# Alpha of the first four chunks loaded as two pairs, five staging tiles and fewer dummy matmuls in a fused linear attention and MLP kernel

## The chip, the core and the metric

The kernel runs on one core of one Trainium2 chip. The metric is the device time of one execution in microseconds (us); less is better. Several executions are timed and one more is profiled.

Engines are called as the profile calls them: PE (TensorE, matmuls; PEld is its weight loads), DVE (VectorE), ACT (ScalarE), POOL (GpSimd), SP (SyncE, which here issues every DMA from one queue, in program order). The on-chip memory has 128 partitions; matmul results go to PSUM banks.

## What is computed

A gated linear attention over 4 x 8 heads, 768 tokens and head width 48 feeds an MLP with a squared ReLU:

```python
B, H, S, D = q.shape            # 4, 8, 768, 48
state = np.zeros((B, H, D, D)); y = np.zeros_like(q)
for t in range(S):
    state = alpha[:, :, t, :, None] * state + np.einsum('bhd,bhe->bhde', k[:, :, t], v[:, :, t])
    y[:, :, t] = np.einsum('bhd,bhde->bhe', q[:, :, t], state)
x = y.transpose(0, 2, 1, 3).reshape(B * S, H * D)     # 3072 x 384
h = np.maximum(x @ w_in, 0.0)                         # w_in 384 x 2048
out = (h * h) @ w_out                                 # w_out 2048 x 384
```

All inputs and the output are float32.

## The kernel before

**Tiling.** The 3072 tokens are 24 chunks of 128, six per batch entry. Each chunk goes through the attention and becomes a block of 128 columns of `xT_big`; the MLP then works on groups of chunks (`GN`: the first group is chunks 0 to 3, then one, one, and pairs). Matmuls are bf16.

**A chunk of the attention** (`add_chunk`). The running product of alpha is a prefix sum of logarithms. ACT takes the logarithm; PE multiplies it with a triangular matrix (op `p0`, the prefix sums); ACT makes `A` = exp and `Ainv` = exp of the negative (L408, L412); DVE multiplies `qA` = q A (L431) and `kI` = k Ainv (L434); PE transposes both (`p1q`, `p1k`, L241); DVE or ACT copies them to `qkT`; PE forms the scores (`p2`, tile `sc`); DVE masks them (`sm`, L472, two halves); POOL has cast v to bf16 (`vb`, L388); PE multiplies scores with v and adds the state's part (`p3a`, `p3b`); ACT evacuates (`xn`), PE transposes (`p4`), and a copy writes `xT_big`. Beside that PE updates the state (`ps`), DVE scales it with `ae` (the exponential of the chunk's total logarithm, L492), ACT casts it (`sb`, L497). `p0`, the transposes, `p3` and `p4` share two PSUM banks (`GLA_BANKS`); the scores have one more tile.

**Alpha of the first four chunks** (`add_joint_alpha`, L312). The 512 tokens of chunks 0 to 3 are laid four to a partition: partition p holds tokens 4p to 4p+3, in pieces of 768 bytes per head. Two DMAs of four heads (L319) fill a tile taken from the staging pool; two logarithms (L324) write `L4`, a view of a tile that the MLP uses later. Chunk s then lies on partitions 32s to 32s+31, so its prefix sum is four matmuls on 32 rows with shifted windows of `tri4` (L397), and 16 small matmuls with `sel4` give the totals of all four chunks at once (`add_totals`, L334), from which two exponentials make `ae` (L342). All four prefix sums wait for both logarithms. From chunk 4 on, alpha is loaded, like q, k and v, as 128 tokens on 128 partitions in pieces of 192 bytes, 192 KB a load (L354).

**Weights** (`load_w`). w_in comes in six loads (cut at f-tiles 0, 2, 4, 6, 8, 12, 16 of 128 columns; 384 KB or 768 KB each), w_out in four of 768 KB. Each lands in a float32 staging tile (pool `stage`, four tiles, of which the joint alpha has one) and is cast to bf16 by POOL, DVE or ACT (L290 to L294). A load waits until the cast four places earlier in `w_cast` has freed its tile.

**MLP.** `add_moe1` makes blocks of 12 matmuls (in the first group: four f-tiles of one chunk, three contraction steps each), a ReLU on ACT (L577) and a square on DVE (L585); `add_moe2` makes four quarters of four f-tiles per chunk, each quarter of the first group needing one w_out load, then an evacuation (L617) and an output DMA.

**Order.** A planner (`Plan.run`) lists the operations with a duration, dependencies, a priority and the PSUM banks they take; it simulates the engines and sorts by planned start, and each engine's instructions are issued in that order. DMAs are one first-in first-out list, `DMA_ORDER`, with planned costs `LD` 0.98 us (chunk load), `JLD` 1.18 us (half of joint alpha), `WLD` 2.1 us (768 KB of weights) and a latency of 2.0 us; the first may start at 0.6 us. Other planned values: a logarithm of joint alpha 0.7 us, ACT's latency 0.14, slack ahead of PE 0.05. A chunk's `p0` may not run more than about three and a half chunks ahead of the MLP (`gate`).

**Dummies.** Until the second MLP layer starts, planned gaps on PE are filled with matmuls on a zero tile `warm`: seven 512 wide at the very start, planned to end at 4.2 us, and then, ahead of each PE operation, a number of 256-wide ones computed from the planned gap (L699), in 0.11 us each.

Of the kernel before, what the change touches and what calls it, by code (L numbers as in the profile page):

```python
# [11 lines left out]
ALU = mybir.AluOpType  # L12
# [127 lines left out]
def kernel(  # L140
# [36 lines left out]
    stage = ctx.enter_context(tc.tile_pool(name="stage", bufs=4))  # L177
# [19 lines left out]
    JN, JP = 4, 32  # L197
    JW = P + JN - 1
    tri4 = consts.tile([P, 192], BF16)
    sel4 = consts.tile([P, 64], BF16)  # L200
    nc.gpsimd.memset(tri4, 1.0)
    nc.vector.memset(sel4, 1.0)
    for c in range(JN):
        blk = slice(JP * c, JP * c + JP)
        nc.gpsimd.affine_select(
            out=tri4[blk, 0:JW], in_=tri4[blk, 0:JW], compare_op=ALU.is_ge, fill=0.0,
            base=-(JN - 1), pattern=[[1, JW]], channel_multiplier=-JN,
        )
    for c in range(JN):
        blk = slice(JP * c, JP * c + JP)  # L210
        nc.vector.memset(sel4[blk, 0:JN], 0.0)
        nc.vector.memset(sel4[blk, c:c + 1], 1.0)
# [18 lines left out]
    L4 = gT_s[:, 0:8, :].rearrange("p (r h) (a d) -> p r (h a) d", r=JN, a=4)  # L231
    nc.gpsimd.memset(L4[:, :, :, D:], 0.0)

# [32 lines left out]
    W_CUT = {"i": [0, 2, 4, 6, 8, 12, 16], "o": [0, 4, 8, 12, 16]}  # L266
    SB = 4
# [39 lines left out]
    EARLY = 4  # L307

    JLD = 1.18
    J = {}  # L310

    def add_joint_alpha():  # L312
        src = alpha[0, :, 0:JN * P, :].rearrange("h (p r) d -> p h (r d)", r=JN)
        hs = [slice(0, H // 2), slice(H // 2, H)]

        def ld(hf):
            if hf == 0:
                J["at"] = stage.tile([P, H, JN * D], FP32, name="at4", tag="stage")
            pin(nc.sync.dma_start(out=J["at"][:, hs[hf], :], in_=src[:, hs[hf], :]))  # L319
        lds = [add("DMA", JLD, lambda hf=hf: ld(hf), lat=2.0, at=0.6) for hf in range(2)]  # L320

        def e_ln(hf):
            t = J["at"][:, hs[hf], :].rearrange("p h (r d) -> p h r d", r=JN)
            pin(nc.scalar.activation(L4[:, :, hs[hf], 0:D].rearrange("p r h d -> p h r d"), t, AF.Ln))  # L324
        J["ln"] = [add("ACT", 0.7, lambda hf=hf: e_ln(hf), lds[hf], prio=-15.0) for hf in range(2)]
        w_cast.append(J["ln"][-1])
        add_totals()

    def add_totals():
        def e_tot():  # L330
            J["tot"] = psum(tot, [P, 512], FP32)
            for p in range(NP):
                for r in range(JN):
                    mm(J["tot"][:, JN * p:JN * (p + 1)], lhsT=L4[:, r, 2 * p:2 * p + 2, :], rhs=sel4[:, 0:JN],  # L334
                       start=(r == 0), stop=(r == JN - 1), skip_group_check=True)
        tot = Op("PE", 0.42, e_tot, J["ln"], prio=-9.9, takes=GLA_BANKS, lat=0.05)
        plan.add(tot)

        def e_ae(j):
            rows = slice(64 * j, 64 * j + 64)  # L340
            t = J["tot"][rows, 0:NP * JN].rearrange("p (n c) -> p c n", c=JN)
            pin(nc.scalar.activation(ae_s[rows, 0:JN, :, j], t, AF.Exp))  # L342
        x0 = add("ACT", 0.19, lambda: e_ae(0), tot, prio=-9.9)
        J["ae"] = add("ACT", 0.19, lambda: e_ae(1), tot, after(x0), prio=-9.9)
        tot.gives = J["ae"]
# [12 lines left out]
    def add_chunk(s):  # L358
# [16 lines left out]
        joint = s < JN  # L375
        jb = slice(JP * s, JP * s + JP)
# [3 lines left out]
        if joint:  # L380
            ln = J["ln"]
        else:
            ln = [add("ACT", 0.41, e_ln, d["ld_at"], old, prio=-15.0 if s < EARLY else -5.0)]
            d["use_at"] = ln[0]
# [7 lines left out]
        def e_p0():  # L392
            pm = d["pm"] = psum(p0, [P, 512], FP32)
            if joint:
                for r in range(JN):
                    mm(pm[:, 0:HD], lhsT=tri4[jb, JN - 1 - r:JN - 1 - r + P], rhs=L4[jb, r, :, 0:D],
                       start=(r == 0), stop=(r == JN - 1))  # L397
                return
# [4 lines left out]
        p0 = Op("PE", 0.66 if joint else 0.27, e_p0, ln, takes=GLA_BANKS, lat=0.05, **g)  # L403
# [18 lines left out]
        if joint:  # L422
            ae1 = J["ae"]
# [6 lines left out]
        def e_qA():  # L430
            pin(nc.vector.tensor_mul(qA[:, :, 0:D], d["qt"], d["A"]))  # L431

        def e_kI():
            pin(nc.vector.tensor_mul(kI[:, :, 0:D], d["kt"], d["Ai"]))  # L434
        mq = d["use_qt"] = add("DVE", 0.47, e_qA, a_, d["ld_qt"], old, **g)
        mk = d["use_kt"] = add("DVE", 0.47, e_kI, ai, d["ld_kt"], old, **g)
# [32 lines left out]
        def e_sm(hh):  # L469
            if hh == 0:  # L470
                d["sm"] = work.tile([P, 2, NP, P], BF16, name="sm")
            pin(nc.vector.tensor_mul(d["sm"][:, hh], d["sc"][:, hh], utri_b.to_broadcast([P, NP, P])))  # L472
        sm0 = add("DVE", 0.6, lambda: e_sm(0), p2, **g)
        sm1 = add("DVE", 0.6, lambda: e_sm(1), p2, after(sm0), **g)
        p2.gives = sm1
# [150 lines left out]
    DMA_ORDER = ["at", (0, "qt"), (0, "kt"), (1, "qt"), (1, "kt"), (0, "vt"), (2, "qt"),  # L626
# [108 lines left out]
```

## Time and profile before

| | us |
|---|---|
| median of 3 timed runs | 191.19 (190.68 to 192.44) |
| profiled execution | 192.79 |
| its span on the core | 191.1 |
| PE busy in the span | 183.5 |
| of it, dummies (57 matmuls, bank<-warm) | 11.5 |
| DVE busy / ACT busy | 128.0 / 123.8 |
| DMA queue, mean share of 16 engines | 66.6% |

The costliest groups on PE are the two MLP layers: 720 matmuls into the first layer (76.8 us busy) and 384 of the second (71.6 us). Busy time of matmuls counts each from issue to its modelled end, and they overlap, so the start-to-start distance is what one costs in a dense run.

"Idle before" and "releaser" name how long an engine sat idle before a group and what ended the wait. Numbers after "x" are counts. A DMA's line on SP is the time its issue took; the transfer lands some microseconds later. The granted clock (PEclk) is in shares of full speed.

Durations used later: a chunk's qA or kI 0.55 us on DVE; one half of the masked scores 0.68; a joint logarithm 0.84 us on ACT; A or Ainv 0.50; a weight cast of 768 KB 0.95 us on DVE, 1.47 on ACT; of 384 KB 0.55 and 0.83.

### The profile page before, as it was taken

What the parts mean: (1) busy time and instruction counts of PE and PEld (TensorE: products, weight loads), DVE (VectorE), ACT (ScalarE), POOL (GpSimd) and SP (SyncE); (2) the same over time, 40 slices, a digit from 0 to 9 for tenths busy, and PEclk for the clock granted to TensorE, in tenths of its full rate; (3) what the DMA queues carried; (4) which work ended last, traced back from release to release, by engine and by line L of the source; (5) the groups of instructions that cost most, each with busy time, mean ns of one, the idle gap of its engine ahead of it and who ended that gap; (6) DMA issues with size and microseconds to landing.
All of it is one profiled execution on the core that took longest, in us unless ns stands there. A gap on an engine that the chain in (4) does not pass through costs nothing.

```text
span 191.1 us, 5257 instructions
## 1 busy us (share of the span) xinstructions
PE 183.5 (96%) x2101; PEld 138.8 (73%) x2101; DVE 128.0 (67%) x277; ACT 123.8 (65%) x285; POOL 18.9 (10%) x43
## 2 busy tenths in 40 slices
PE   7898999889999999999999999999999999999992
PEld 2577899557886788857868868868868768768651
DVE  1178899654898999858758768767857858735100
ACT  4475799346896778946955955946946746728221
POOL 8121100101111111112110110010010000000000
PEclk9999999999999999999999999999999999999999
DMA  6999898999989999999999999650110110111112
GB/s 182 212 232 274 282 282 191 284 310 186 229 183 224 217 198 199 224 180 223 191 231 238 177 232 196 129 151 0 46 41 0 46 41 5 41 41 45 38 51 78
DMA packets 104730, 30.23 MB, mean 158 GB/s; under 512 B 96257, under 2 KB 103937, under 8 KB 104705
## 3 DMA queue, kind: packets, MB, share of 16 engines
q1 hardware_dynamic: 104704, 29.89, 66.6%
q8 instruction: 16, 0.26, 0.6%
q14 instruction: 10, 0.07, 0.1%
HBM read 25.17 MB, written 4.72 MB: 156 GB/s over the span
## 4 chain that ended last, share of the span: by engine, by line
PE 82%; DMA 8%; ACT 3%; DVE 2%; SPq 2%; issue 1%; POOL 0%; POOLq 0%
PE bank L238 69%; PE bank L241 7%; PE sc L238 4%; DMA wo<-in_moe_w_out_dram 3%; DMA at<-in_alpha_dram 2%; DMA vt<-in_v_dram 2%; SPq L354 2%; PE st L238 2%; DVE gT L585 1%; DVE w_out_b L292 1%; ACT r L577 1%; DVE w_in_b L292 0%; ACT ob L617 0%; ACT qkT L369 0%; ACT L_s L379 0%
## 5 line engine op out<-in xcount | busy, mean ns | idle before, releaser
L238 PE MATMUL bank<-xT_big,w_in_b 128*128 128x256 bf16 (+1 forms) x720 | 76.8, 251 | 0.0
L238 PE MATMUL bank<-w_out_b,gT 128*128 128x384 bf16 x384 | 71.6, 326 | 1.2 <-DVE w_out_b L292 1.2
L577 ACT ACTIVATE r<-bank 128x512 bf16<-128x512 f32 x96 | 56.4, 603 | 16.5 <-PE bank L238 14.2
L238 PEld LDWEIGHTS <-w_in_b 128*128 128x128 bf16 x720 | 55.5, 98 | 5.0
L238 PEld LDWEIGHTS <-gT 128*128 128x128 bf16 x400 | 35.6, 97 | 20.2 <-issue 1.2
L585 DVE TENSOR_TENSOR gT<-r 128x512 bf16<-128x512 bf16 x96 | 38.8, 429 | 14.6 <-ACT r L577 14.4
L472 DVE TENSOR_TENSOR sm<-sc,utri_b 128x512 bf16<-128x512 f32 x48 | 30.8, 683 | 3.3 <-PE sc L238 3.3
L388 POOL CAST vb<-vt 128x384 bf16<-128x384 f32 x24 | 14.2, 592 | 121.6 <-DMA vt<-in_v_dram 71.7
L431 DVE TENSOR_TENSOR qA_s<-qt,A 128x384 bf16<-128x384 f32 x24 | 13.3, 552 | 19.1 <-ACT A L408 19.1
L617 ACT COPY ob<-bank 128x384 f32<-128x384 f32 x23 | 11.0, 478 | 22.3 <-PE bank L238 22.2
L371 DVE COPY qkT<-bank 128x1024 bf16<-128x1024 bf16 (+1 forms) x23 | 15.0, 655 | 6.5 <-PE bank L241 6.5
L238 PEld LDWEIGHTS <-qkT 64*128 64x128 bf16 (+1 forms) x272 | 10.9, 95 | 6.8 <-issue 2.0
L408 ACT ACTIVATE A<-bank 128x384 bf16<-128x384 f32 x24 | 11.9, 497 | 4.9 <-PE bank L238 4.7
L434 DVE TENSOR_TENSOR kI_s<-kt,Ainv 128x384 bf16<-128x384 f32 x24 | 14.8, 615 | 0.2 <-DMA kt<-in_k_dram 0.2
L497 ACT CAST sb<-st 128x384 bf16<-128x384 f32 x20 | 9.6, 479 | 7.4 <-DVE st L492 7.3
L379 ACT ACTIVATE L_s<-at 128x384 bf16<-128x384 f32 x20 | 10.4, 522 | 5.8 <-DMA at<-in_alpha_dram 5.7
L238 PE MATMUL bank<-warm 128*128 128x256 bf16 (+1 forms) x57 | 11.5, 346 | 1.3 <-DVE warm L186 1.3
L369 ACT CAST xn<-bank 128x384 bf16<-128x384 f32 x24 | 11.6, 482 | 1.7 <-PE bank L238 1.7
L412 ACT ACTIVATE Ainv<-bank 128x384 bf16<-128x384 f32 x24 | 12.0, 499 | 0.0
L492 DVE TENSOR_TENSOR st<-st,ae_s 128x384 f32<-128x384 f32 x20 | 11.1, 556 | 0.0
L241 PE MATMUL bank<-ident_bf,kI_s 128*128 128x128 bf16 x96 | 9.3, 219 | 0.5 <-ACT qkT L369 0.5
L238 PEld LDWEIGHTS <-warm 128*128 128x128 bf16 x57 | 6.0, 114 | 5.2 <-issue 2.8
(52 smaller groups left out, 141.3 us busy)
## 6 DMA issues: line engine op xcount, KB each, us to landing
qt<-in_q_dram SPq DMA_DIRECT2D x24, 192.0 KB, 3.8
kt<-in_k_dram SPq DMA_DIRECT2D x24, 192.0 KB, 3.8
vt<-in_v_dram SPq DMA_DIRECT2D x24, 192.0 KB, 4.0
out_dram<-ob SPq DMA_DIRECT2D x24, 192.0 KB, 2.6
at<-in_alpha_dram SPq DMA_DIRECT2D x20, 192.0 KB, 4.0
wo<-in_moe_w_out_dram SPq DMA_DIRECT2D x4, 768.0 KB, 6.6
wi<-in_moe_w_in_dram SPq DMA_DIRECT2D x4, 384.0 KB, 5.7
wi<-in_moe_w_in_dram SPq DMA_DIRECT2D x2, 768.0 KB, 6.4
```

The lines of the kernel that those rows point to most:

```text
L238: pin(nc.tensor.matmul(*a, **kw))
L241: pin(nc.tensor.transpose(*a))
L369: pin(nc.scalar.copy(out_t, in_t))
L371: pin(nc.vector.tensor_copy(out_t, in_t))
L388: pin(nc.gpsimd.tensor_copy(d["vb"], d["vt"]))
L408: pin(nc.scalar.activation(d["A"], d["pm"][:, 0:HD].rearrange("p (h d) -> p h d", h=H), AF.Exp))
L412: pin(nc.scalar.activation(d["Ai"], d["pm"][:, 0:HD].rearrange("p (h d) -> p h d", h=H), AF.Exp, scale=-1.0))
L431: pin(nc.vector.tensor_mul(qA[:, :, 0:D], d["qt"], d["A"]))
L434: pin(nc.vector.tensor_mul(kI[:, :, 0:D], d["kt"], d["Ai"]))
L472: pin(nc.vector.tensor_mul(d["sm"][:, hh], d["sc"][:, hh], utri_b.to_broadcast([P, NP, P])))
L577: pin(nc.scalar.activation(box["r"][:, 0:w], box["ph"][:, 0:w], AF.Relu))
L585: pin(nc.vector.tensor_mul(gT[g][:, f0:f0 + per, lo * P:lo * P + n], r, r))
```

## The change

Alpha of chunks 0 to 3 is loaded as two pairs (0, 1) and (2, 3), with two tokens per partition (pieces of 384 bytes), one DMA of 384 KB and one logarithm each. The tables `tri` and `sel` are made for pairs, with 64 rows per chunk; a chunk's prefix sum is two matmuls on 64 rows, and each pair has its own totals (8 small matmuls) and exponentials. Alpha lands in a tile `Aj` of its own, in space that an MLP tile uses later, and not in the staging pool, which grows from four tiles to five. w_in has five loads instead of six (f-tiles 4 to 8 in one). `DMA_ORDER` puts pair 0 ahead of q, k, v of chunks 0 and 1, pair 2 ahead of those of chunks 2 and 3, and all w_in loads behind these. The count of dummies in each gap ahead of 19 us is rounded down from the planned gap (0.0 in place of 0.9 added). Planned costs: 1.4 us and a latency of 2.05 for a pair, from 0.8 us on.

The diff also adds ways to put some products on POOL or ACT (`QE`, `KE`, `SMP`); their tables are empty, so these branches don't run.

```diff
-    stage = ctx.enter_context(tc.tile_pool(name="stage", bufs=4))
+    stage = ctx.enter_context(tc.tile_pool(name="stage", bufs=5))
...
-    JN, JP = 4, 32
...
+    JSETS = [(0, 2), (2, 2)]
+    tri_j, sel_j = {}, {}
+    for n in sorted({n for _, n in JSETS}):
+        tri_j[n] = consts.tile([P, 192], BF16, name=f"tri{n}")
+        sel_j[n] = consts.tile([P, 64], BF16, name=f"sel{n}")
+        nc.gpsimd.memset(tri_j[n], 1.0)
+        nc.vector.memset(sel_j[n], 0.0)
+        for x in range(n):
+            blk = slice(P // n * x, P // n * (x + 1))
+            nc.gpsimd.affine_select(
+                out=tri_j[n][blk, 0:P + n - 1], in_=tri_j[n][blk, 0:P + n - 1], compare_op=ALU.is_ge, fill=0.0,
+                base=-(n - 1), pattern=[[1, P + n - 1]], channel_multiplier=-n,
+            )
+            nc.vector.memset(sel_j[n][blk, x:x + 1], 1.0)
...
+    Aj = big.tile([P, H, 4 * D], FP32, name="gT1", tag="gT1")
...
-    W_CUT = {"i": [0, 2, 4, 6, 8, 12, 16], "o": [0, 4, 8, 12, 16]}
-    SB = 4
+    W_CUT = {"i": [0, 2, 4, 8, 12, 16], "o": [0, 4, 8, 12, 16]}
+    SB = 5
...
-    JLD = 1.18
+    JLD = {2: 1.4, 4: 2.36}
...
+    def add_joint_alpha(s0):
+        n = dict(JSETS)[s0]
+        b, c = divmod(s0, NCH)
+        src = alpha[b, :, c * P:(c + n) * P, :].rearrange("h (p r) d -> p h (r d)", r=n)
+        A, L = Aj[:, :, s0 * D:(s0 + n) * D], Lj[:, s0:s0 + n]
+        hs = [slice(x * H // (n // 2), (x + 1) * H // (n // 2)) for x in range(n // 2)]
...
+        for h in hs:
+            x = add("DMA", JLD[n] / len(hs), lambda h=h: ld(h), lat=2.05, at=0.8)
+            lns.append(add("ACT", 0.7, lambda h=h: e_ln(h), x, prio=-15.0))
...
+            for p in range(NP):
+                for r in range(n):
+                    mm(box["tot"][:, n * p:n * (p + 1)], lhsT=L[:, r, 2 * p:2 * p + 2, :], rhs=sel_j[n][:, 0:n],
+                       start=(r == 0), stop=(r == n - 1), skip_group_check=True)
+        tot = plan.add(Op("PE", 0.104 * n, e_tot, lns, prio=-9.995 + s0 * 0.01, takes=GLA_BANKS, lat=0.05))
...
-            if joint:
-                for r in range(JN):
-                    mm(pm[:, 0:HD], lhsT=tri4[jb, JN - 1 - r:JN - 1 - r + P], rhs=L4[jb, r, :, 0:D],
-                       start=(r == 0), stop=(r == JN - 1))
+            if j:
+                n, jb = j["n"], j["blk"]
+                for r in range(n):
+                    mm(pm[:, 0:HD], lhsT=tri_j[n][jb, n - 1 - r:n - 1 - r + P], rhs=j["L"][jb, r, :, 0:D],
+                       start=(r == 0), stop=(r == n - 1))
...
-    DMA_ORDER = ["at", (0, "qt"), (0, "kt"), (1, "qt"), (1, "kt"), (0, "vt"), (2, "qt"),
-                 (2, "kt"), (1, "vt"), (2, "vt"), "i", (3, "qt"), (3, "kt"), "i", (3, "vt"),
-                 "i", "i", "i", "i", "o", 4, "o", "o", "o", 5]
+    DMA_ORDER = ["0", (0, "qt"), (0, "kt"), (0, "vt"), (1, "qt"), (1, "kt"), (1, "vt"), "2", (2, "qt"), (2, "kt"), (2, "vt"), (3, "qt"), (3, "kt"), (3, "vt"), "i", "i", "i", "i", "i", "o", 4, "o", "o", "o", 5]
...
-                n = max(0, int((op.start - pe_end) / 0.11 + (0.9 if op.start < DENSE else -1.8)))
+                n = max(0, int((op.start - pe_end) / 0.11 + (0.0 if op.start < DENSE else -1.8)))
```

## Prediction

> **What bounds the kernel now.** The page first: the engines' shares and the 40 slices.
>
> ```profile
> PE 183.5 (96%) x2101; PEld 138.8 (73%) x2101; DVE 128.0 (67%) x277; ACT 123.8 (65%) x285; POOL 18.9 (10%) x43
> ...
> DMA  6999898999989999999999999650110110111112
> ```
>
> PE is busy 96% of the span, so the time can only fall by what PE does uselessly or idly. The group of dummies (bank<-warm, x57) holds 11.5 us of that busy time, all before 20 us. Next the busy times by stretch:
>
> ```profile
> core 0: us, PE busy (x) PEld busy (x) DVE busy (x) ACT busy (x) POOL busy (x), PEclk, DMA share, GB/s
> 0.00:7.44 7.44, 6.13 (x23) 2.98 (x23) 0.86 (x11) 2.97 (x3) 4.65 (x19) 1.00 0.82 195
> 7.44:20.00 12.56, 11.47 (x156) 8.41 (x155) 9.45 (x19) 8.42 (x19) 1.95 (x3) 1.00 1.06 253
> 20.00:26.00 6.00, 5.89 (x111) 5.21 (x109) 5.32 (x12) 4.95 (x12) 0.60 (x1) 1.00 0.85 260
> 26.00:36.00 10.00, 10.00 (x159) 9.12 (x157) 9.00 (x20) 8.47 (x19) 0.51 (x1) 1.00 0.88 219
> 36.00:39.00 3.00, 1.77 (x23) 1.11 (x22) 1.99 (x3) 0.00 (x0) 0.00 (x0) 1.00 1.07 391
> ```
>
> The reader is to see that PE is full from 26 us on, but for one hole at 36 to 39 us. Before 7.44 it has only dummies. So the change is worth as much as it pulls forward the dense first-layer stretch, plus that hole. The chain in order of time names the hole's cause:
>
> ```profile
> 30.89 0.40 DVE w_out_b L292
> 31.29 6.38 DMA wo<-in_moe_w_out_dram
> 37.70 0.97 DVE w_out_b L292
> 38.71 3.24 PE bank L238 x28
> ```
>
> The second w_out load is issued at 31.29, lands at 37.7 and is cast; PE resumes at 38.71. Why so late is in SP's queue (timeline and waits of SP):
>
> ```profile
> 15.74 6.47 SPq L286 DMA_DIRECT2D wi<-in_moe_w_in_dram  x4
> 24.33 0.37 SPq L286 DMA_DIRECT2D wo<-in_moe_w_out_dram  x1
> 24.75 0.50 SPq L354 DMA_DIRECT2D at<-in_alpha_dram  x1
> ...
> 27.21 3.33 SPq L354 DMA_DIRECT2D kt<-in_k_dram  x1
> ```
>
> ```profile
> SPq L286 <- ACT w_in_b L294: 2.8, 2, 2.0
> SPq L286 <- DVE w_in_b L292: 2.5, 1, 2.5
> ```
>
> SP waits 5.3 us for casts, that is for staging tiles: the fifth w_in load goes at 18.52 after the first cast (ends 18.48), the sixth at 21.84 after the second, the first w_out at 24.33 after the third. Meanwhile the DMA share is 0.85 to 0.88, and everything behind in the one queue, chunk 4 and w_out included, comes later. By issue time plus time to landing, w_in's last load lands at 28.6, w_out's first at 30.7, its second at 37.7, its last at 42.2.
>
> **The change, part by part.** *Transfer prices from landings.* The two alpha halves land at 4.1 and 5.35 (their logarithms start at 4.11 and 5.36), v of chunk 1, eight loads on, at 12.5: 0.89 us per chunk load. The 384 KB weights at 21.2 and 22.3: 1.1. The w_out loads at 37.7, 40.0, 42.2: 2.25 per 768 KB when queued back to back.
>
> *Alpha in pairs.* 384-byte pieces are not in the trace. Bounds for one 384 KB pair: below, the half of 768-byte pieces, 1.25; above, two chunk loads of 192-byte pieces, 1.78. I take 1.4, nearer the first, since a fixed cost per piece is spread over twice the bytes of the small ones. Pair 0 lands at 4.4 (4.1 to 4.7). Both pairs cost 2.8 against 2.5, so DMA is 0.3 us (0 to 1.1) worse off. The Trainium skill ("DMA: Bandwidth & Descriptors", Specifications) speaks against this: it puts line rate at pieces of 512 B and more, with a read-modify-write below. By it one would take the upper price, and the sum below would give 2.7 instead of 3.5; no run so far shows which.
>
> *Start.* The planner places the first prefix matmul at 0.8 + 1.4 + 2.05 + 0.7 + 0.14 + 0.05 = 5.14, formerly 0.6 + 2.36 + 2.0 + 0.89 = 5.85. Dummies ahead of it: int(0.94/0.11) = 8, formerly int(1.65/0.11 + 0.9) = 15. The seven wide ones end at 4.48, the fifteen took 2.96 us, 0.197 each, so the prefix starts at 4.48 + 8 x 0.197 = 6.1 instead of 7.44, 1.3 us sooner; its logarithm (0.84 us) is done by 5.3.
>
> *Prefix sums and totals.* Two matmuls per chunk instead of four: 8 x 0.16 = 1.3 us less PE work, and totals are again 16 tiny matmuls, in two sets. The first set now stands between chunks 0 and 1 and takes one of two banks, so chunk 1's prefix waits on PE for chunk 0's second exponential. Queued behind it are chunk 0's transposes. I put it at 7.9; A of chunk 1 follows at 8.4 (9.05 before), so this wait costs nothing.
>
> *Order of loads.* v0 moves ahead of q1 and k1, both early w_in loads behind v3. Landings at the prices above: six loads to 9.75, pair 2 at 11.15, six more to 16.5 (v3; 20.2 before), w_in at 17.6, 18.7, 20.95, 23.2, 25.45, w_out's first at 27.7, chunk 4 at 31.25, w_out's others at 33.5, 35.75, 38.0. The first w_in load comes 2.2 us later than before (15.4); its cast ran at 17.65 to 18.48 anyway and would now end near 18.6: no cost. Chunk 2's logarithm waits for pair 2 at 11.15 on ACT; behind it are chunk 1's copies, which the planner orders by readiness. Before, chunk 2's A came at 10.06, now near 12.7, but its qA ran only at 13.98 and can still do so.
>
> *Five staging tiles, alpha in a tile of its own.* All five w_in loads go without a wait; w_out's first needs the first cast (18.6), long done when SP gets there. This removes the 5.3 us of waits.
>
> *Fewer dummies, shorter set-up.* Each gap loses about one dummy; two fewer selects on POOL (0.35 each) and six small DVE memsets were done by 3.5 us, ahead of the first use. Nothing on the path, if the clock holds (a rival below).
>
> *The sum.* First-layer groups of four f-tiles need 4 x 12 matmuls at 0.0556 = 2.67 us each (18 in 1.34 us less the last one's drain, in the timeline at 24.18). The third w_in load, cast by 21.9, opens groups 1 to 3: 8.0 us, with the fifth cast by 26.5, before group 3 begins at 27.2. Chunk 3 must be ready: its kI can run at 15.9; from kI to xT took 6.2 us (19.89 to 26.07), so 22.1. PE reaches the second layer at 29.9, with 0.4 of chunk 4 at 30.3, against 33.74: 3.4 us. From there to the hole lie 3.55 us of work: 33.9; w_out's second load is cast at 33.5 + 1.0 = 34.5, against 38.71: 4.2 us. That assumes full queues. Before, o1 to o2 took 6.9 us for 4 x 0.89 + 2.25 = 5.8, a loss of 1.1 beside the 3.33 us issue of kt; that stretch of the queue remains. I charge 0.7 of it: **3.5 us**. DVE, 90% busy from 26 to 36, is late next; it carries the same squares and casts, 1.3 us sooner started. The profiled run took 192.79 (span 191.1): 189.3. The median of the runs shown is 1.6 under that run: 191.2 - 3.5 = **187.7**.
>
> Bounds of my case: 5.3 gained (no queue loss, alpha at 1.25, weights at 2.0, as 391 GB/s moves them: third w_in cast by 21.35, PE at the hole at 33.4) and 2.4 (1.1 lost, both pairs at 1.78): 185.9 to 188.8.
>
> **Rivals.** *Given back.* A of chunks 5 to 9 starts at 44.5, 48.8, 53.9, 59.6, 63.6, some 4.8 us apart, later 7.0: there chunks arrive just in time at a DMA share of 1.0. If later loads, waiting for buffers and output stores, keep only part of the lead, PE stalls at 45 to 70 us. For it: the pace; against it: chunk 4 and 5 gain the same lead. If 1.5 us remain: 189.7.
>
> *The queue gains nothing.* w_in's fifth and sixth loads landed 4.2 us apart. If weights queued five deep still need 3.1 us each, the 4.2 us are used up by five loads ahead of the hole (0.84 each): 191. Against it: 2.25 for the w_out loads queued together.
>
> *Slower: the clock.* PEclk reads 1.00 throughout, yet fifteen 256-wide dummies took 0.197 each before 7.44 and nine at 16.21 took 0.11: PE ran at half rate until about 7 us. With dummies thinned, PE may stay or fall back there. Place: 7 to 22 us, 9.8 us of full-rate work (attention of four chunks 7.1 by its counts at the later pitches, group 0 2.67), 8.6 of it in matmuls long enough to double. At half rate that is 18.4, from 6.1 to 24.5, 2.6 after the weights, and the next 1.7 us of dense work double before the clock returns: gain 3.5 - 4.3, and a further 1.0 if chunk 3 lags by it: 193. It decides only if half rate lasts beyond some 15 us; before that, waits for chunks 2 and 3 hide it. Against it: no dummy starts between 14.3 and 16.2 us and the nine at 16.21 still run at 0.11. The Trainium skill ("TensorE: Matmul & The Clock Gate", Part 1) has full rate come with one busy window of about 3.4 us and go with an idle one of that length; by it this rival would not occur and 187.7 would stand.
>
> **How the numbers follow.** My case 0.67, given back 0.12, queue 0.10, clock 0.11. The range 185.9 to 190.2 takes my case's bounds and the first rival's, and leaves out the clock and most of the queue rival, about 0.19. About 1% (1.9 us) is what a measurement tells from no change. Faster by more: my case and half of the first rival, 0.73; within: the other half, most of the queue rival and the mildest clock, 0.15; slower 0.12.
>
> **What would show it.** 15 warm matmuls in the first run of them, first prefix near 6.1; alpha's first pair landed near 4.4, the second near 11.2; no SP wait on a w_in cast; w_in's last load landed near 25.5, w_out's second near 33.5 to 34.5; first second-layer matmul near 30; no PE hole over 0.5 us at 33 to 36; later A's some 3.5 us sooner each. Wrong if dummies of 0.2 appear after 8 us, if 768 KB loads land over 3 us apart, or if PE idles at 45 to 70.

## The result and the profile after

The changed kernel takes 192.35 us (median of 20 runs, 191.0 to 194.46), the kernel before on the same chip 191.32 (20 runs): the ratio is 1.0049, 95% interval 1.0028 to 1.0071. A gain of 3.5 us was forecast; what came is a loss of about 1 us, inside the 1% that was called no change. The profiled execution took 192.70 us, its span 190.6. Two things about these numbers. The profiled execution of the kernel before (192.79) is 1.5 us above that kernel's median, so the two traces do not show the difference of the medians. And the time outside the span (device time less span) is 2.0 us on average in the 20 executions of the changed kernel, and 1.72 in the 135 of the kernel before in the jobs of the experiments: some 0.3 us of the loss lies outside the span, where no view of the trace shows what it is.

The page of the changed kernel, the engines' shares and the row of the DMA engines in 40 slices:

```profile
PE 183.8 (96%) x2109; PEld 139.3 (73%) x2109; DVE 129.8 (68%) x276; ACT 120.7 (63%) x281; POOL 18.6 (10%) x41
...
DMA  6998997999999997999999999660110110111012
```

The dummies, meant to be fewer, are 73 with 13.8 us (57 with 11.5 before). Ahead of the first prefix there are 15 (22 before); after it 58 (35 before). The busy times by the same stretches as before:

```profile
core 0: us, PE busy (x) PEld busy (x) DVE busy (x) ACT busy (x) POOL busy (x), PEclk, DMA share, GB/s
0.00:7.44 7.44, 6.13 (x31) 2.83 (x31) 0.76 (x6) 2.93 (x5) 4.50 (x18) 1.00 0.80 171
7.44:20.00 12.56, 11.97 (x157) 8.95 (x156) 10.46 (x22) 7.57 (x20) 2.19 (x4) 1.00 0.97 209
20.00:26.00 6.00, 4.76 (x89) 4.25 (x88) 5.07 (x11) 2.84 (x6) 0.00 (x0) 1.00 1.00 348
26.00:36.00 10.00, 10.00 (x172) 9.55 (x170) 9.11 (x20) 8.71 (x18) 0.66 (x1) 1.00 0.92 251
36.00:39.00 3.00, 2.99 (x31) 1.86 (x30) 2.73 (x6) 0.14 (x2) 0.00 (x0) 1.00 1.06 390
```

The hole at 36 to 39 us is gone (2.99 of 3.00 busy, 1.77 before), and a hole of the same size stands at 20 to 26 us (4.76 of 6.00, 5.89 before). It stands 13 us earlier, and nothing was won by that. The timeline of PE shows its place in the changed kernel ("[...]" is the idle time before a group and what ended it):

```profile
23.69 0.49 PE L237 MATMUL bank<-xT_big,w_in_b 128*128 128x128 bf16 x6
25.42 0.38 PE L237 MATMUL bank<-warm 128*128 128x256 bf16 x2 [1.24 <-ACT r L593]
25.63 0.33 PE L240 MATMUL bank<-ident_bf,xn 128*128 128x128 bf16 x3
25.80 2.40 PE L237 MATMUL bank<-xT_big,w_in_b 128*128 128x128 bf16 x40
```

and in the kernel before, at the same time:

```profile
24.18 1.34 PE L238 MATMUL bank<-xT_big,w_in_b 128*128 128x128 bf16 x18
25.35 0.33 PE L241 MATMUL bank<-ident_bf,xn 128*128 128x128 bf16 x3
25.52 2.69 PE L238 MATMUL bank<-xT_big,w_in_b 128*128 128x128 bf16 x44
```

Before, 18 first-layer matmuls fill the time until chunk 3's tokens (`xn`) are there. In the changed kernel two f-tile pairs of w_in have been used up for the three chunks at hand, the next piece is cast on DVE only at 23.87 to 24.82, and two dummies stand at the head of PE's queue. They write the PSUM bank that a first-layer block holds, so they wait for ACT's ReLU of that block, and chunk 3's transposes wait behind them, with `xn` done since 24.48. The cast, `xn` and the ReLU:

```profile
23.87 0.95 DVE L291 CAST w_in_b<-wi 128x1536 bf16<-128x1536 f32 x1
24.01 0.47 ACT L373 CAST xn<-bank 128x384 bf16<-128x384 f32 x1
24.74 0.63 ACT L593 ACTIVATE r<-bank 128x512 bf16<-128x512 f32 x1
```

The rows of the queue. The issues of SP in the changed kernel (each line's second number is how long the issue took):

```profile
15.54 3.09 SPq L285 DMA_DIRECT2D wi<-in_moe_w_in_dram  x5
...
22.12 5.45 SPq L358 DMA_DIRECT2D qt<-in_q_dram  x1
27.61 3.47 SPq L358 DMA_DIRECT2D kt<-in_k_dram  x1
31.13 1.03 SPq L358 DMA_DIRECT2D vt<-in_v_dram  x1
32.26 1.92 SPq L285 DMA_DIRECT2D wo<-in_moe_w_out_dram  x3
```

All five w_in loads go out without a wait from 15.54 on. The next load, w_out's first, needs the tile of w_in's first, and SP waits for it from 18.63 to 21.07: 1.1 us until that load lands, 1.3 more until it is cast.

```profile
SPq L285 <- DVE w_in_b L291: 1.3, 1, 1.3
SPq L285 <- DMA wi<-in_moe_w_in_dram: 1.1, 1, 1.1
```

So 2.4 of the 5.3 us of waits for staging tiles remain. Then the issue of chunk 4's q takes 5.45 us (1.86 before) and its k 3.47 (3.33). SP comes to chunk 4's v at 31.13; before, at 30.58. What was won in waits went into long issues; five tiles alone, below, do the same (3.47 and 3.99 for that q and k). That SP is held there by a queue that is full is a reading; the trace names no cause. By issue time plus time to landing, pair 0 is there at 4.3, v of chunk 1 at 9.8, pair 2 at 12.3, v of chunk 3 at 17.9, w_in at 19.7, 21.5, 23.8, 25.9, 29.2, w_out's second load at 37.5.

The second layer starts at 34.77 (33.74 before), its 17th matmul at 38.50 (38.71), right behind the cast of w_out's second load, and the last matmul of all at 186.97 (187.11).

```profile
37.48 0.96 DVE L291 CAST w_out_b<-wo 128x1536 bf16<-128x1536 f32 x1
38.50 1.46 PE L237 MATMUL bank<-w_out_b,gT 128*128 128x384 bf16 x8
```

### The profile page after: what moved, and what is told of

Same layout as the page of the kernel before. It is cut to its first block, busy times and chain, and to the rows that moved or that the text cites. A ratio compares the mean times of both kernels' runs of the same rounds, so it can differ in the third digit from the quotient of the medians.

```text
span 190.6 us, 5256 instructions
## 1 busy us (share of the span) xinstructions
PE 183.8 (96%) x2109; PEld 139.3 (73%) x2109; DVE 129.8 (68%) x276; ACT 120.7 (63%) x281; POOL 18.6 (10%) x41
## 4 chain that ended last, share of the span: by engine, by line
PE 71%; DMA 16%; DVE 4%; ACT 3%; SPq 2%; issue 1%; POOL 1%; POOLq 0%; DVEq 0%; ACTq 0%
PE bank L237 60%; DMA wo<-in_moe_w_out_dram 9%; PE bank L240 6%; DMA vt<-in_v_dram 5%; PE sc L237 3%; DMA at<-in_alpha_dram 2%; SPq L358 2%; PE st L237 1%; DVE sm L476 1%; ACT w_out_b L293 1%; POOL vb L391 1%; DVE kI_s L438 1%; ACT A L412 1%; DVE w_out_b L291 1%; DVE qkT L375 0%
## 5 line engine op out<-in xcount | busy, mean ns | idle before, releaser
L593 ACT ACTIVATE r<-bank 128x512 bf16<-128x512 f32 x96 | 56.6, 603 | 18.6 <-PE bank L237 16.1
L601 DVE TENSOR_TENSOR gT<-r 128x512 bf16<-128x512 bf16 x96 | 39.0, 429 | 13.9 <-ACT r L593 13.6
L391 POOL CAST vb<-vt 128x384 bf16<-128x384 f32 x24 | 14.5, 604 | 122.3 <-DMA vt<-in_v_dram 74.9
L435 DVE TENSOR_TENSOR qA_s<-qt,A 128x384 bf16<-128x384 f32 x24 | 13.7, 573 | 17.9 <-ACT A L412 17.9
L633 ACT COPY ob<-bank 128x384 f32<-128x384 f32 x22 | 10.5, 477 | 22.6 <-PE bank L237 22.6
L375 DVE COPY qkT<-bank 128x1024 bf16<-128x1024 bf16 (+1 forms) x26 | 16.2, 628 | 7.3 <-PE bank L240 7.1
L237 PE MATMUL bank<-warm 128*128 128x256 bf16 (+1 forms) x73 | 13.8, 319 | 2.5 <-DVE ae_s L226 1.3
L438 DVE TENSOR_TENSOR kI_s<-kt,Ainv 128x384 bf16<-128x384 f32 x24 | 13.8, 576 | 0.0
L237 PEld LDWEIGHTS <-warm 128*128 128x128 bf16 x73 | 7.1, 106 | 6.1 <-issue 3.9
L375 DVE COPY xT_big<-bank 128x384 bf16<-128x384 bf16 x23 | 8.1, 351 | 3.2 <-PE bank L240 3.1
```

What stands on the lines that cost most here:

```text
L237: pin(nc.tensor.matmul(*a, **kw))
L375: pin(nc.vector.tensor_copy(out_t, in_t))
L391: pin(nc.gpsimd.tensor_copy(d["vb"], d["vt"]))
L435: pin((nc.gpsimd if mq.eng == "POOL" else nc.vector).tensor_mul(qA[:, :, 0:D], d["qt"], d["A"]))
L438: pin((nc.gpsimd if mk.eng == "POOL" else nc.vector).tensor_mul(kI[:, :, 0:D], d["kt"], d["Ai"]))
L593: pin(nc.scalar.activation(box["r"][:, 0:w], box["ph"][:, 0:w], AF.Relu))
```

## The experiments

Names: "b" kernels start from before, "a" kernels from the changed one. Each ratio is against the kernel before on the same chip in the same job; that kernel's median was 192.56 in the first four runs, 193.09 in the next four, then 191.5, 191.4 and 191.52. "17th" is the second layer's 17th matmul, the first that needs w_out's second load.

**Is it the staging tiles, the order, or the dummies?** Five tiles alone, on before:

```diff
-    stage = ctx.enter_context(tc.tile_pool(name="stage", bufs=4))
+    stage = ctx.enter_context(tc.tile_pool(name="stage", bufs=5))
-    SB = 4
+    SB = 5
```

> The kernel before with a fifth staging tile and the cast it waits for five places back, nothing else. Staging theory (the prediction's): the 5.3 us of waits on casts go, w_in's last load lands at 26 to 27 instead of 28.6, the second w_out load near 34 to 35, the hole at 37 us closes: 1.5 to 3.5 us faster. Queue theory: the DMA engines and the issue queue already move the first 30 us at the rate they can, a free tile only lets more wait in line; w_in's last load lands within 0.7 us of 28.6 and the time stays within 0.7 us.

Measured: 192.26 us, 0.9970 (0.9934 to 1.0006). The second layer starts at 32.8 and the 17th comes 0.9 us sooner than in the trace of before. Even that is not shown to come from the tiles. b_ln and b_ln2 below have four tiles and, up to 60 us, the same instructions in the same order as before; there w_out's second load lands at 36.5 (37.7 in before), against 36.8 here and 37.6 in b5_ln, which has five. One early program so differs by 1.2 us from trace to trace, and five tiles are worth nothing beyond that; the 4.2 us of the prediction they are not. In this trace chunk 11's A is still 1.3 us sooner than before's (76.5 against 77.8), chunk 12's 0.3 (84.6 against 84.9). In between stands this, on ACT and on PE:

```profile
83.46 0.52 ACT L379 ACTIVATE L_s<-at 128x384 bf16<-128x384 f32 x1 [3.37 <-DMA at<-in_alpha_dram]
```

```profile
84.78 0.34 PE L241 MATMUL bank<-ident_bf,xn 128*128 128x128 bf16 x3 [1.08 <-ACT xn L369]
```

ACT runs in order, and chunk 14's logarithm stands ahead of the copies that PE needs for chunk 12. It waits 3.37 us for chunk 14's alpha; PE then idles 1.08 us. The kernel before comes there later and waits less:

```profile
83.77 0.52 ACT L379 ACTIVATE L_s<-at 128x384 bf16<-128x384 f32 x1 [2.40 <-DMA at<-in_alpha_dram]
```

In the changed kernel the same logarithm starts at 83.53 after a wait of 2.47 us. Alpha of chunk 14 is loaded in a stretch in which the DMA share reads 0.95 to 1.04 in both kernels (20-us stretches from 40 to 120 us), which may be why it does not come sooner when PE leads. In the seven kernels that have this wait (0.8 to 3.4 us), chunk 12's A starts at 84.5 to 85.4, though their chunk 4's starts at 32.6 to 34.9.

The changed order and the five cuts of w_in on before; the reverse on the changed kernel; and the changed kernel with the old count of dummies:

```diff
-    W_CUT = {"i": [0, 2, 4, 6, 8, 12, 16], ...
+    W_CUT = {"i": [0, 2, 4, 8, 12, 16], ...
-    DMA_ORDER = ["at", (0, "qt"), (0, "kt"), (1, "qt"), ...
+    DMA_ORDER = ["at", (0, "qt"), (0, "kt"), (0, "vt"), (1, "qt"), ...
```

> The kernel before (alpha of four chunks as one set, four staging tiles, its dummies) with the changed order of loads alone: q, k, v of chunks 0 to 3 first, then five w_in loads. Order theory (weights behind all chunk loads start the first layer late and chunk 3 is not ready sooner): w_in's first load lands after 19 us instead of 15.4, the dense stretch starts later, 0.7 to 2 us slower than before. If the order is harmless and something else of the change costs: within 0.5 us of before.

> The changed kernel (pairs, five tiles, fewer dummies) with the order and cuts of before: six w_in loads, two of them ahead of v of chunk 3, pair 2 ahead of q of chunk 2. Order theory: w_in's first load lands at 15 to 17 us again, the time falls 1 to 2 us below the changed kernel's, to about before's or 0.5 us under it. Piece theory (alpha in 384-byte pieces costs the time): stays 0.7 to 1.5 us above before.

```diff
-   n = max(0, int((op.start - pe_end) / 0.11 + (0.0 if op.start < DENSE else -1.8)))
+   n = max(0, int((op.start - pe_end) / 0.11 + (0.9 if op.start < DENSE else -1.8)))
```

> The changed kernel with the dummies rounded as before (0.9 added). Clock theory: fewer dummies cost clock or readiness, so 0.5 us or more faster than the changed kernel. Otherwise: PE waits for data in this stretch, a dummy more in each gap delays the operation behind by up to 0.1 us here and there: within 0.4 us of the changed kernel.

Measured: b_order 1.0002 (0.9963 to 1.0041), a_order 1.0063 (1.0022 to 1.0105), a_dum 1.0027 (0.9987 to 1.0068). The number of dummies makes nothing that can be told from the changed kernel's own 1.0049. The order alone puts the second layer at 35.2 in place of 33.7, with the time as it was, and the old order on the changed kernel doesn't bring it back (35.1): there PE idles 1.94 us near 25.6, on a dummy that waits for a bank.

**The wait near 85 us taken away.** The planner issues by planned times; a longer planned latency for the alpha loads from chunk 10 on puts chunk 14's logarithm behind chunk 12's A:

```diff
-        d["ld_" + nm] = add("DMA", LD if s < 4 else LD1, ld, prev, lat=2.0 if s < 4 else 2.4, at=0.6)
+        d["ld_" + nm] = add("DMA", LD if s < 4 else LD1, ld, prev, lat=2.0 if s < 4 else (4.4 if nm == "at" and s >= 10 else 2.4), at=0.6)
```

On before, on the changed kernel, on before with five tiles; and, without this edit, the changed kernel with no dummies planned after 19 us (`and op.start < DENSE` added to the condition):

> The kernel before, planned latency of alpha's load 4.4 us instead of 2.4 from chunk 10 on, nothing else: in ACT's order the logarithm of chunk 14 moves from ahead of chunk 12's evacuation, xn and A to behind them. Pin theory (in every run so far PE comes to the same point near 85 us, since ACT sits in that logarithm waiting for a load that lands at 83.4 to 83.7): ACT's wait ahead of xn near 81 to 84 us goes and A of chunk 12 starts below 84.5; with little lead before it, 0 to 0.7 us faster. Order theory (only the early order counts): no change, within 0.3 us.

> The changed kernel with the same shift of logarithms from chunk 10 on. Pin theory: A of chunk 12 below 84.5, the few tenths that the changed kernel leads by at 42 us reach the end: 0.2 to 0.8 us below the changed kernel. Order theory: no change from the changed kernel.

> The kernel before with five staging tiles and the same shift of logarithms. With five tiles alone PE led by 0.9 us at 38 to 77 us and lost all of it near 84. Pin theory: the lead survives, A of chunk 12 near 83.5, the end 0.8 to 1.3 us under before, 0.5 to 1.0 under five tiles alone. If the lead is lost anyway to loads that come no sooner (DMA theory): PE holes at 86 to 100 us instead, time as with five tiles alone.

> The changed kernel without any dummy after the planned 19 us (it has a few at 20 to 26 us; the two at 25.42 wait for a ReLU to free their bank and hold chunk 3's last transposes behind them). Dummy-bank theory: the hole of 1.2 us near 24 to 25.4 shrinks, xT of chunk 3 ends 0.5 to 1 us sooner, the second layer starts 0.5 to 0.9 us sooner; by the pin theory little of it reaches the end: 0 to 0.5 us. If these dummies do not matter: xT of chunk 3 stays at 26.4.

Measured: b_ln 0.9915 (0.9884 to 0.9946, six executions), a_ln 1.0026 (0.9999 to 1.0054), b5_ln 0.9921 (0.9896 to 0.9947), a_late0 1.0032 (1.0003 to 1.0061). ACT's waits for alpha near 85 us are gone in the three, and the two kernels now lie 1.1% apart, in favour of before. Five tiles add nothing to b_ln. Without the late dummies the hole shrinks to 0.36 us and the second layer starts 0.7 us sooner (34.07), and chunk 12's A still comes at 85.4.

**What of the change costs the 1.1%?** All with the wait taken away (5.0 us in place of 4.4 for the first two):

> The kernel before, with the changed kernel's order of loads and its five cuts of w_in, and with the planned latency of the alpha loads from chunk 10 on raised (to 5.0 us, the smallest value that puts chunk 14's logarithm behind chunk 12's A on ScalarE), so that the wait near 85 us can't even the kernels out. The same edit of the latency alone gave 0.9915 of before. Theory 'the order costs it' (w_in later, chunk 3's tokens later): second layer's 17th matmul near 39 us, last matmul near 187, time 0.5 to 0.8% above the 0.9915, so 0.997 to 1.000. Theory 'the pairs cost it' (pair 2's pieces of 384 bytes in the middle of the queue): within 0.3% of 0.9915, 17th matmul by 38.0. Theory 'late dummies on a block's bank cost it': also within 0.3%, since this kernel has before's start, except where such a dummy shows.

> The changed kernel with the alpha of the first four chunks as one set of four tokens per partition again (768-byte pieces, both halves first in the queue), its order of the other loads and five staging tiles kept, and the wait near 85 us lifted (latency 5.0). The changed kernel with that wait lifted gave 1.0026, before with it lifted 0.9915. Theory 'the pairs cost it': most of the 1.1% comes back, 0.992 to 0.996, last w_in about 1 us sooner than in the changed kernel. Theory 'the order costs it': little comes back, 0.998 to 1.003, the second layer's 17th matmul near 39. Theory 'late dummies': little comes back unless no such dummy stands ahead of chunk 3's transposes in its trace.

> The changed kernel with before's order of loads and its six cuts of w_in (pair 2 ahead of chunk 2's q), five tiles and the pairs kept, and the wait near 85 us lifted. Theory 'the order costs it': 0.993 to 0.997, the second layer's 17th matmul near 38. Theory 'the pairs cost it': no better than the 1.0026 of the changed kernel with that wait lifted. Theory 'late dummies': 1.00 or above, since this order showed 1.94 us of PE idle on a dummy's bank near 25.6 us.

> The changed kernel without the dummy matmuls that are planned after 19 us, and with the wait near 85 us lifted. Without these dummies alone chunk 3's transposed tokens came 0.73 us sooner and the second layer began 0.7 us sooner, and all of that was lost again at the wait. Theory 'late dummies cost it': 0.4% under the 1.0026 of the changed kernel with the wait lifted, so 0.998 to 1.000, and the last matmul near 186.8; if they were the whole of the 1.1%, 0.992 to 0.995. Theories 'pairs' and 'order': 1.000 to 1.003.

Measured: 1.0052 (1.0024 to 1.0079), 1.0036 (1.0006 to 1.0066), 1.0097 (1.0058 to 1.0136), 1.0069 (1.0044 to 1.0093). None of the theories takes all: the order on before costs 0.6% (against b_ln2, below, on another chip with the same time of before), the quad put back on the changed kernel saves 0.3% (against a_ln2, below), no more than the intervals allow for chance, and without the late dummies nothing is saved in the time. One thing was not expected at all. The busy times of a_order_ln by stretch:

```profile
24.00:26.00 2.00, 0.51 (x14) 0.45 (x12) 1.45 (x4) 2.00 (x5) 0.00 (x0) 1.00 1.01 344
26.00:27.00 1.00, 0.55 (x9) 0.54 (x9) 0.00 (x0) 0.40 (x1) 0.00 (x0) 0.96 1.05 395
27.00:28.00 1.00, 1.00 (x12) 1.00 (x11) 0.58 (x2) 0.00 (x0) 0.00 (x0) 0.50 1.05 388
28.00:30.00 2.00, 2.00 (x22) 2.00 (x20) 1.34 (x4) 1.19 (x2) 0.00 (x0) 0.50 1.08 237
```

PE was idle for 1.94 us up to 26.45, on the dummy's bank, and from 26.9 to 30.3 the granted clock (third number from the end) is 0.50. The second layer starts at 37.3. Five of this kernel's ten executions took 192.1 to 192.5 us at a mean clock of 0.997 to 1.0, the other five 194.3 to 194.6 at 0.991; the ratio of 1.0097 takes both together, and the first five alone lie some 0.5% above before. So the clock of the third rival does fall, but behind a hole in PE's work and not because dummies are few. The hole alone does not settle it. The first line is a_order_ln's, the second a_order's, whose trace has no fall:

```profile
26.45 0.27 PE L237 MATMUL bank<-warm 128*128 128x256 bf16 x1 [1.94 <-ACT r L593]
25.61 0.27 PE L237 MATMUL bank<-warm 128*128 128x256 bf16 x1 [1.94 <-ACT r L593]
```

In a_order_ln's trace the granted clock changes at 6.43, 26.91 and 30.32 us: six steps of 3.413 us, then one. Counted in such steps, its hole lies in the one from 23.50 to 26.91, in which PE is busy 1.47 us, and the clock falls at its end. In a_order, counted from 4.59, where its granted clock starts, a step ends at 25.07 inside the hole, and the two steps have 2.01 and 2.76 us of work. The two traces thus fit a clock that is set by how busy PE was in the last step; where the limit lies between 1.47 and 2.01 us of 3.41, they do not show.

**Both kernels without the wait on one chip, and the first layer's work as the measure.** On the changed kernel with the old order, and on the changed kernel with the quad (latency 5.0), the late dummies are left out:

> The kernel before with only the planned latency of the alpha loads from chunk 10 on raised to 4.4 us, again, on another chip. Its 0.9915 was measured where the kernel before took 193.1 us; elsewhere the kernel before took 191.3 to 191.5. Theory 'the wait near 85 us costs the kernel before 0.9% everywhere': 0.988 to 0.995. Rival 'that wait is only as long as the chip's alpha transfers are late': 0.995 to 1.000 where the kernel before is near 191.4, and 0.99 where it is near 193.

> The changed kernel with the same raised latency, beside the run above, so that the two kernels stand on one chip without that wait. Theory 'the changed kernel is behind when the second layer starts, because fewer first-layer matmuls are started by 26 us (36 to 40 against 60 to 63 in the traces), and nothing makes it up': 1.0 to 1.2% above the kernel before with the raised latency on this chip. Rival 'the 1.1% was that chip's': within 0.4% of it.

> The changed kernel (pairs, five tiles) with before's order of loads, without the dummies planned after 19 us, with the raised latency. Theory 'what counts is how many first-layer matmuls are started by 26 us': w_in is there from 16 to 19 us and no dummy waits for a bank ahead of chunk 3's transposes, so 50 to 60 of them by 26 us (36 and 41 with the dummies), the second layer's first matmul 33.8 to 34.3, and a time 1.0 to 2.0% under the 1.0097 that the same kernel has with the dummies. Rival 'the hole stays, since chunk 3 isn't there': under 45 by 26 us, first second-layer matmul above 34.8. Theory 'clock': with the hole filled by real work or ended sooner, the half clock from 26.9 to 30.3 us that the kernel with the dummies shows is gone; without the dummies' cover it could also come more often: then 1.01 and a granted clock of 0.991.

> The changed kernel with the quad of alpha back at the head of the queue, the changed order, five tiles, no dummies planned after 19 us, raised latency. With those dummies it had 58 first-layer matmuls started by 26 us, the second layer's first matmul at 33.75 and 1.0036. Theory 'first-layer matmuls by 26 us': the dummy's 0.69 us wait on a bank goes, 64 to 70 by 26 us, first second-layer matmul 33.1 to 33.5, time 0.2 to 0.4% less, 0.999 to 1.002, or less still if nothing stalls at 60 to 78 us, where the kernel with the dummies lost 1.8 us. Rival 'clock': a granted clock of 0.991 in some runs and 0.5% more.

Measured: b_ln2 0.9988 (0.9963 to 1.0013), a_ln2 1.0063 (1.0037 to 1.0089), a_order_late0_ln 1.0101 (1.0062 to 1.0140, median 192.46), a_j4_late0_ln 1.0018 (0.9993 to 1.0043). So the wait near 85 us costs before nothing measurable on a chip where it takes 191.4 us, and 0.85% on the one where it takes 193.1: no version here is shown to beat both kernels everywhere. The changed kernel without the wait is behind on both chips, by 0.75% here. The traces show where: against b_ln2 the A's of a_ln2 lag by 0.7 us at chunks 4 to 7 and by 1.7 from chunk 9 on (PE waits 0.65 us at 63.44 for ACT's `sb`), and the lag stays to the end. The 1.0101 of a_order_late0_ln rests on three executions of 193.8 to 194.4; the other four took 190.9 to 192.5, 0.3% above before on average.

**Is the queue the limit?** w_out's second load ahead of chunk 4's four loads, on b_ln and on a_order_late0_ln:

```diff
-                 "i", "i", "i", "i", "o", 4, "o", "o", "o", 5]
+                 "i", "i", "i", "i", "o", "o", 4, "o", "o", 5]
```

> The kernel before with the raised latency (0.9988 alone on one chip, 0.9915 on another) and one more edit: w_out's second piece ahead of chunk 4's four loads in the queue. Theory 'the queue carries a fixed number of bytes before w_out's second piece, and the second layer's 17th matmul waits for that piece': it lands some 2.6 us sooner (34.5 to 35.5 instead of 36.5 to 37.7), the 17th comes at 36.9 to 37.4, as soon as PE can be there, instead of 37.7 to 38.7, and chunk 4's loads land 2 us later. If chunk 4 doesn't mind: 0.4 to 0.6% less, 0.992 to 0.995. Rival 'chunk 4 then is the one that is late': its A after 36 instead of 33.5, the hole comes back at 36 to 45 us, 0.998 to 1.005.

> The changed kernel with before's order, without the dummies planned after 19 us, with the raised latency (median 192.46 there, first second-layer matmul at 33.4), and with w_out's second piece ahead of chunk 4's loads. Theory 'queue': w_out's second piece lands at 34.0 to 35.0, the 17th second-layer matmul at 36.7 to 37.2 (37.8 without the edit); if what the change makes ready sooner can be used at all, this is the form of it that shows it: 0.990 to 0.996 of the kernel before. Rival 'chunk 4 is late', or 'what is gained by 37 us is lost at 60 to 95 us': within 0.5% of 1 or above.

Measured: 0.9994 (0.9958 to 1.0031) and 1.0048 (1.0018 to 1.0077). The load lands at 33.2 and 32.6 and the 17th follows to 36.1 and 36.2, so there the queue's order decides. But chunk 4's A comes at 35.6 (33.5 in b_ln2), w_out's third load at 39.4 after all (38.6 in b_ln2), and PE waits for that cast, and later for chunk 5's tokens, which come 0.7 us later too. PE of b_o2_ln:

```profile
40.39 1.46 PE L238 MATMUL bank<-w_out_b,gT 128*128 128x384 bf16 x8 [0.62 <-DVE w_out_b L292]
...
52.40 0.83 PE L238 MATMUL bank<-xT_big,w_in_b 128*128 128x128 bf16 x12 [0.54 <-DVE xT_big L371]
```

What the order gives to one load it takes from the next.

All kernels by their traces (times in us; "L1" is the number of first-layer matmuls started before 26 us):

```
kernel             w_in  w_in    L1    second  w_out  17th  last     ratio to
                   1st   last          layer   2nd          matmul   before
before             15.4  28.6    60    33.7    37.7   38.7  187.1
b_stage5           15.9  27.8    75    32.8    36.8   37.8  187.4    0.9970
b_order            19.3  26.5    47    35.2    36.0   38.6  187.1    1.0002
b_ln               15.9  27.9    63    33.5    36.5   37.7  185.5    0.9915
b_ln2              15.4  28.0    60    33.7    36.5   37.9  185.4    0.9988
b5_ln              15.7  27.4    60    33.7    37.6   38.6  186.5    0.9921
b_order_ln         19.4  28.4    43    35.2    37.3   38.6  188.0    1.0052
b_o2_ln            14.9  28.9    64    33.2    33.2   36.1  187.1    0.9994
after              19.7  29.2    40    34.8    37.5   38.5  187.0    1.0049
a_dum              19.4  28.1    36    35.3    36.8   38.9  187.0    1.0027
a_order            16.8  28.4    41    35.1    37.5   39.3  187.3    1.0063
a_late0            19.4  28.8    53    34.1    37.0   38.0  187.7    1.0032
a_ln               19.9  30.4    36    35.1    38.6   39.6  187.5    1.0026
a_ln2              18.8  29.0    36    35.0    37.5   38.7  187.2    1.0063
a_late0_ln         19.4  29.0    46    34.4    38.1   39.1  186.7    1.0069
a_j4_ln            18.0  26.8    58    33.7    35.7   37.4  185.9    1.0036
a_order_ln         16.3  26.9    36    37.3    36.8   41.5  189.1    1.0097
a_order_late0_ln   16.8  28.1    65    33.4    36.7   37.8  185.5    1.0101
a_j4_late0_ln      17.8  27.4    64    33.5    37.0   38.1  186.8    1.0018
a_o2_ln            17.0  28.3    62    33.3    32.6   36.2  186.3    1.0048
```

Two readings. The first: from 26 us on PE runs the first layer without a gap at 0.0556 us a matmul, so the second layer starts at 33.7 + (60 - L1) x 0.0556: 34.8 for the changed kernel's 40, 32.9 for 75, 33.4 for 65, as measured. Three kernels lie well above the line: the two with the changed order on before (by 0.5 to 0.8) and a_order_ln, which has the half clock. The others are within 0.4 us of it. One early program can differ by 15 here (75 in b_stage5, 60 in b5_ln), so only the larger differences count. And the second layer's start does not settle the time: b_order starts it at 35.2 and takes as long as before. The second reading: the 17th matmul comes no sooner than 1.0 us after w_out's second load landed, in every kernel.

## Why the prediction was wrong, step by step

**The landings: wrong, and the step that failed.** "This removes the 5.3 us of waits" was to bring w_out's second load from 37.7 to 33.5 and with it 4.2 us at the hole. The load landed at 37.5. The prediction read SP's waits as the cause of the late loads; but the DMA engines were at work in them: in its three waits (17.65 to 18.52, 18.89 to 21.84 and 22.21 to 24.33 us) their share is 1.06, 0.94 and 0.78. The same 8.65 MB (sixteen chunk loads, w_in, two loads of w_out, chunk 4) are landed by 37.7 us before and 37.5 after. With five tiles alone the load comes at 36.8 and 37.6, with four at 36.5 to 37.7. Nor did the waits all go: "long done when SP gets there" was wrong too, for w_in's first load landed at 19.7 and not at 17.6, and 2.4 us of waits remained. From w_in's last load on the forecast holds: 8.3 us to w_out's second, forecast 8.05. Nearly all of the delay stands before that.

**Prices.** 0.89 us per chunk load held up to v of chunk 1 (9.8 forecast 9.75). Behind it two terms were too small. Up to v of chunk 3: 17.9 instead of 16.5. Pair 0 landed at 4.3 as said, but pair 2, in the middle of the queue, took 2.57 us instead of 1.4 (1.75 to 2.2 in the nine other kernels with pairs, nearly all above the upper bound of 1.78); the three loads behind it made up half of that, and q of chunk 3 took 2.1. Then the five w_in loads, queued without a gap, took 1.8, 1.7, 2.3, 2.15 and 3.3 us, 11.3 in all instead of 8.95. So w_in's last came at 29.2 instead of 25.5. The Trainium skill ("DMA: Bandwidth & Descriptors", Specifications) puts line rate at 512 bytes and more. Per piece the trace shows no step there (median times 15 ns for 192 bytes, 22 for 384, 36 for 768, 65 for 1536). In the changed order the pairs do cost: w_in's last load is at 26.8 and 27.4 with the quad and five tiles, and at 28.1 to 30.4 in the six kernels with pairs. In the order of before, with five tiles, it is 27.4 and 27.8 with the quad and 26.9 to 28.4 with pairs. The pieces are the same in both orders, so their length alone is not shown to be the cause.

**Start: right, and worth nothing.** Fifteen warm matmuls, the first prefix at 6.10, chunk 1's at 7.55, chunk 0's `xT` at 13.6 (16.8 before). But chunk 2's A came at 14.5 (forecast 12.7), and "chunk 3 at 22.1" was wrong: 26.4, as before (26.1). Its q and k land later (16.5 and 17.3, before 16.1 and 16.8) and the dummies hold it.

**w_in at 17.6 "no cost": wrong.** This is the edit that was costed at nothing, with cover that was not there: w_in early is what fills PE's gaps between chunks, and with it at 19.7 only 40 first-layer matmuls are started by 26 us (36 in a_ln and a_ln2, the same early program) instead of 60: 20 x 0.0556 = 1.1 us, which is the 1.03 us by which the second layer starts later. The late dummies are part of it: they were put into the gap that the missing work leaves in the plan. Without them it is 53 and 46 (a_late0, a_late0_ln) and the second layer starts 0.6 to 0.7 us sooner. With before's order besides, w_in at 16.8, it is 65 (a_order_late0_ln), so w_in's time and what else the order moves are the rest.

**The rivals.** "Queue gains nothing" is what happened, at 192.35 a little worse than its 191; 0.10 was too little for it. Its price of 3.1 us for 768 KB only w_in's last load had (3.3; the other two 2.3 and 2.15). "Given back" is right in kind: in the traces leads of up to 1.3 us were lost, near 84 us and not at 45 to 70, on ACT behind chunk 14's alpha. The same wait may also hide part of the change's own loss: 0.5% with it, 0.75 to 1.1% without, but on different chips and with intervals that overlap. "Clock" as stated is false: the granted clock is 1.00 from 5.9 us on (7.0 before), 4.6 us after PE's first matmul, which agrees with the Trainium skill's one busy window. Its rule for falling back, an idle window of about 3.4 us ("TensorE: Matmul & The Clock Gate", Part 1), doesn't hold here: in a_order_ln the clock fell behind a stretch of 3.41 us in which PE was busy 1.47 us.

**Open.** Why the gain didn't come is answered by the landings; the loss of 1 us is accounted for only in part. 0.3 us of it lies outside the span. The changed kernel and the five others with both pairs and the changed order have 1.9 to 2.0 us there, all the rest 1.7 to 1.8; no trace shows why. The later second layer explains the lag of a_ln2 at chunk 4, but b_order has a later one still and loses nothing. a_order_late0_ln has 65 first-layer matmuls by 26 us and its profiled run of 190.9 us ends like b_ln2's; where its three long executions lose 2 to 3 us, no trace shows. Why pair 2 takes 2 us and more in the queue was not settled either: 1024 pieces of 22 ns on 16 engines would be 1.4 us, as forecast, and the rate falls to 30 GB/s near 12.5 us with no cause that the trace names. Nor was it settled why w_in's loads take longer here than the 1.1 and 2.25 us that were read off before's weight loads.

## What to carry to other kernels

A wait for a buffer ahead of a DMA is worth only what the queue has free in the meantime: read the DMA share and the length of the issues behind the wait, and add up the bytes up to the load that matters, before counting the wait as time to win. Before a difference of 1 us between two traces is read as an effect, it helps to look at two traces of one early program: here they differ by as much. A load moved back "at no cost" needs the list of what the engine would have done with it; here the first layer's matmuls filled gaps that then stood empty. And a lead is worth nothing if an engine that runs in order has a wait for a paced transfer ahead of the work the others need: look for that place downstream first.

## What was not expected of the hardware

- Most SP issues take 0.4 to 1.2 us; in the stretch with the weight loads those of chunk 4's and chunk 5's q and k take 1.9 to 5.5. The wait is then in the issue and in no list of waits.
- The granted clock falls to 0.50 for 3.4 us in the trace of a_order_ln, and the two kernels with a hole of 1.94 us in PE's work have the mean clock of that execution (0.991) in 5 of 12 and 5 of 10; it costs some 2 us. It is not theirs alone: 9 of 135 executions of the kernel before have a mean clock of 0.987 to 0.991.
- A dummy matmul can cost more than the gap that it fills, when its PSUM bank is in use: 1.24 us in the changed kernel, 1.94 in a_order.
